# Three widths for the last two experts, and five banks for the last output rows, in an attention and MoE kernel

## The chip, the cores and the metric

The kernel runs on one core of a Trainium2 chip. A core has five engines with an instruction stream each: TensorE (PE), VectorE (DVE), ScalarE (ACT), GpSimd (POOL) and SyncE (SP), beside DMA engines. Matmuls write to PSUM, in banks of 128 partitions x 512 words of 32 bits. The metric is the device time of one execution in microseconds. Three timed runs of the kernel before gave 481.39, 474.83 and 478.11 us; the median is 478.11.

## The reference

Two parts. First an attention over 4 batches, 8 heads, 576 positions and 64 dimensions each: the sum of an attention over keys averaged by fours, and of an attention within a band of seven positions. Its output is `x`, 4 x 576 tokens of 512 values. Then a mixture of experts with one expert for each token:

```
for b in range(B):
    for s in range(S):
        e = argmax(logits[b, s]) if s == 0 or local_gate[b, s] < 0.5 else prev_e
        p = softmax(logits[b, s])
        h = maximum(x[b, s] @ w1[e], 0)        # 512 -> 1024
        out[b, s] = p[e] * (h @ w2[e])         # 1024 -> 512
        prev_e = e
```

There are 8 experts and 2,304 tokens. How many tokens an expert gets depends on the data. All of it is in fp32.

## The kernel before

The attention writes `x` to DRAM and the routing makes lists of tokens. Then come nine passes, one for each slot, in the order 0, 8, 1, 2, ..., 7. Slot 0 holds expert 0's tokens of the first three batches, slot 8 those of the last, and slots 1 to 7 the other experts, sorted by their number of tokens, most first. Slot 7 is the last pass, and has the fewest. Counted from the reference's inputs, slots 1 to 7 have 397, 330, 291, 274, 269, 214 and 165 tokens.

A product of fp32 matrices is done as three products of parts: `h` is the number rounded to the engine's fp32r, `l` the rest, and the three are h·h, h·l and l·h. ScalarE makes `h`, VectorE or GpSimd makes `l`.

One pass, say for slot e:

- SyncE loads the expert's `w1` and `w2`, ScalarE, VectorE and GpSimd split them (`conv`, L1067 and L1072). GpSimd gathers the slot's tokens in tiles of 128 rows, PE transposes them (L1119).
- First product, `mm1` (L1183): the hidden layer transposed, 8 column blocks `f` of 128 hidden units. A block is 12 matmuls into one PSUM bank, each with a weight tile of 128 x 128 and with n tokens as columns. ScalarE takes `hh` out of the bank (L1192, Relu), VectorE `hl` (L1196), which frees the bank.
- Second product, for all slots but 8 and the last, `mm2t` (L1289): the output transposed, 4 blocks of 24 matmuls, again n columns wide. VectorE copies it to `oT` (L1297), and PE transposes it back by tiles of 128 tokens (L1306) into banks of kind O.
- For slot 8 and the last slot, 7, the second product is `mm2` (L1329): rows of 128 tokens x 512, 24 matmuls for each tile, in a branch on whether the tile has any token. An empty tile runs one tiny matmul instead (`idle`, L1076, 128 x 4).
- `gated`: ScalarE scales a tile into `ot` (L1265), and GpSimd writes its rows to the output by an indirect DMA (L1269). This is done for every tile, empty ones too.

How wide n is, PE decides at run time. `LEAVES` lists the widths of each slot, and `sized` (L1162) makes a binary tree of branches on the token count whose leaves hold the matmuls for one width each. The program has such a tree for every two column blocks of the first product and for every block of the transposed second.

PSUM has five banks of kind H, for the transposed tokens and both column products, and two of kind O, for output tiles. `xcount` hands out the banks of a kind in turn, in the order in which the program records the work. A list scheduler (`order`) then sets the order of the instructions on every engine, by the cost of the path behind an operation and a priority of its slot. Each engine executes its list in order, with semaphores between the engines; an instruction that waits holds up all behind it on its engine.

The last pass orders its four tiles 3, 2, 0, 1:

```
mm2(e, o + 2, range(TILES[e]) if nx is not None else (3, 2, 0, 1))
```

Of the kernel before, what the change touches and what calls it, by code (L numbers as in the profile page):

```python
# [9 lines left out]
F32 = mybir.dt.float32  # L10
# [4 lines left out]
AF = mybir.ActivationFunctionType  # L15
# [7 lines left out]
B, H, S, D = 4, 8, 576, 64  # L23
# [7 lines left out]
ZROW = S * SPLIT // NT  # L31
SD = S // 4
LEAVES = [(256, 320, 384), (368, 400, 448, 512), (336, 368, 400, 512), (304, 336, 368, 512), (288, 304, 336, 512),
          (256, 288, 320, 512), (256, 272, 304, 512), (256, 272, 288, 512)]
TILES = [3, 4, 4, 4, 4, 4, 4, 4, 2]
NP = 120
THR = float(np.float32(-1.5 * 2.0 ** -23))
# [268 lines left out]
def attn_moe_kernel(ctx: ExitStack, tc: tile.TileContext, q, k, v, wg, wl, w1, w2, cst, idc, out, info=None):  # L306
    nc = tc.nc
    V, A, G, T, SY = nc.vector, nc.scalar, nc.gpsimd, nc.tensor, nc.sync
# [66 lines left out]
    def t(key):  # L375
        if key not in tiles:
            tag = key[0]
            if tag == "row":
                tiles[key] = pools["row0"][(2 * key[1] + key[2]) % 2]
            elif tag == "vw":  # L380
                tiles[key] = pools["vwb"][(2 * key[1] + key[2]) % 2]
            elif tag == "bd":
                tiles[key] = pools["bdb"][(2 * key[1] + key[2]) % 2]
            elif tag == "psr":
                tiles[key] = pools["psr"]
            elif tag == "ps":
                tiles[key] = pools["ps"].tile([128, 512], F32, tag=f"b{pl.bank_of[key]}", name="ps")
            else:
                sh, dt, bufs = spec[{"h0": "w1h", "w2": "w2r"}.get(key[1], tag)]
                tiles[key] = pools[gof[tag]].tile(sh, dt, tag=tag, name=tag, bufs=bufs)  # L390
        return tiles[key]
# [11 lines left out]
    gi = const.tile([128, 4, NV, 4], U32, name="gi")  # L403
# [24 lines left out]
    def apart(ins, group):  # L428
        tc.declare_no_dep(ins.ins, group=group, reason="rows are disjoint")
        tc.add_to_no_dep_group(group, ins.ins)  # L430
# [592 lines left out]
    def pk_(e, nm, x):  # L1023

        if e == 0 and nm + x in ("w1h", "w2r"):
            return ("w2r", "h0") if nm == "w1" else ("w1r", "w2")
        return (nm + x, e)

    def part(e, nm, x):
        return t(pk_(e, nm, x))  # L1030
# [44 lines left out]
    def idle():  # L1075
        T.matmul(pools["psr"][:, 448:452], wm, wm[:, 0:4], start=True, stop=True)  # L1076

    def half(e):
        return "A" if e == 0 else "B"
# [60 lines left out]
    def xcount(g, kind, n):  # L1140
        if g not in seen:
            seen[g] = bankn[kind] % n
            bankn[kind] += 1
        return seen[g]

    def mb(kind, g):
        return pools[kind][seen[g]]
# [109 lines left out]
                                    t(("hh", e))[:, 4 * q:4 * q + 4, 128 * tl:128 * tl + 128].bitcast(F32), ALU.subtract)  # L1257
                op("DVE", 602, prio + 0.2, lo, R=[g, sl, ("hhp", e, 2 * tl + q)], U=[("hh", e)], W=[("hl", e), ("hlt", e, tl)])

    def gated(e, tl, g, sl, prio):  # L1260

        ok = ("ot", e, tl)

        def ev():
            A.activation(t(ok), mb("O", g), AF.Copy, scale=gi[:, tl, e, 2:3].bitcast(F32))  # L1265
        op("ACT", 580, prio, ev, R=[g, sl, ("gi", half(e))], W=[ok])

        def st():
            ins = G.indirect_dma_start(out, bass.IndirectOffsetOnAxis(ap=gi[:, tl, e, 1:2], axis=0), t(ok), None,  # L1269
                                       bounds_check=NTOK - 1, oob_is_err=False)  # L1270
            apart(ins, "out")
        op("Pool", 1050, prio, st, R=[ok], W=[("out", e, tl)], lat=3000)

    def mm2t(e, prio, tprio):
# [24 lines left out]
        for tl in range(TILES[e]):  # L1299
            g = ("ps2", "o", e, tl)  # L1300
            sl = ("ps2f", "O", xcount(g, "O", 2))

            def tr(tl=tl, g=g):
                def go():
                    for db in range(4):
                        T.transpose(mb("O", g)[:, 128 * db:128 * db + 128], t(ok)[:, db, 128 * tl:128 * tl + 128], ident)  # L1306
                if tl < 2:
                    go()
                    return
                with tc.If(regs[e] > 128 * tl) as cmp:  # L1310
                    go()
                with cmp.Else():
                    idle()
            op("PE", 430, tprio + 0.1 * tl, tr, cnt=1024, R=[ok, ("reg", e)], W=[g, sl])
            gated(e, tl, g, sl, tprio + 0.1 * tl)

    def mm2(e, prio, tiles_):
        for n, tl in enumerate(tiles_):
            g = ("ps2", "o", e, tl)
            sl = ("ps2f", "O", xcount(g, "O", 2))  # L1320

            def fn(tl=tl, g=g):
                hh, hl = t(("hh", e)), t(("hl", e))
                wh, wlo = part(e % E, "w2", "h"), part(e % E, "w2", "l")
                with tc.If(regs[e] > 128 * tl) as cmp:
                    i = 0
                    for f in range(8):
                        for a, c in ((hh, wh), (hh, wlo), (hl, wh)):
                            T.matmul(mb("O", g), a[:, f, 128 * tl:128 * tl + 128], c[:, f], start=(i == 0), stop=(i == 23))  # L1329
                            i += 1  # L1330
                with cmp.Else():
                    idle()
            hd = [("hht", e, tl), ("hlt", e, tl)] if e == 8 else [("hh", e), ("hl", e)]
            op("PE", 5150 if tl < TILES[e] - 1 else 100, prio + 0.1 * n, fn, cnt=12000, most=0, U=[("hh", e), ("hl", e)],
               R=hd + [pk_(e % E, "w2", "h"), pk_(e % E, "w2", "l"), ("reg", e)], W=[g, sl, ("ord", seq_.index(e))])

            gated(e, tl, g, sl, prio + 0.1 * n)

    seq_ = [0, 8, 1, 2, 3, 4, 5, 6, 7]
    load_w1(0, 117)  # L1340
# [12 lines left out]
    for i, e in enumerate(seq_):  # L1353
        o = M + 10 * i
        nx = seq_[i + 1] if i + 1 < NV else None
        if nx is not None:
            if i:
                load_w1(nx, o)
            if i > 1:
                load_w2(nx, o + 0.1)  # L1360
            if i == 0:
                gather(8, 134)
                gather(1, 134.5)
            elif i > 1:
                gather(nx, o)
            count(nx, o - 9)
        (mm1x if e == 8 else mm1)(e, o)
        if i == 1:
            load_w2(nx, o + 0.1)
        if nx is not None:  # L1370
            x_T(nx, o + 1)
            if i:
                conv(nx, "w1", o + 2)
        if e < E and nx is not None and 1:
            mm2t(e, o + 2, o + 10.05)
        else:
            mm2(e, o + 2, range(TILES[e]) if nx is not None else (3, 2, 0, 1))
        if nx is not None and i:
            conv(nx, "w2", o + 4)
# [77 lines left out]
```

## Time and profile before

| | |
|---|---|
| median of three timed runs | 478.11 us (474.83 to 481.39) |
| profiled execution, its own time | 473.6 us |
| its span | 471.8 us |
| mean granted clock of TensorE | 0.943 |
| PE busy | 410.7 us, 87% |
| DVE, ACT, POOL busy | 62%, 54%, 48% |
| slot 6's second product, first to last matmul | about 415.65 to 427.22 us |
| slot 7's first product | 427.22 to 439.43 us |
| slot 7's output rows, tiles 0 and 1 | 442.01 to 455.0 us |
| last store of the passes | 456.09 us |

The busy shares are means over the whole span, with stages of different limits. What the change touches lies in the last fifth, so the timeline and the tables by stage of that part are the ones to read. Idle time of an engine is followed in brackets by what ended it, as far as the profile could tell. Matmuls are pipelined: the length shown for one is longer than the distance to the start of the next, and the distance is what counts.

### The profile page before, as it was taken

The page shows a single profiled execution, that of the slowest core. Times are in us where ns is not written, and L with a number is a line of the kernel's source. Part 1 is how long each engine was busy: PE and PEld are TensorE (multiplying, and loading weights), DVE is VectorE, ACT ScalarE, POOL GpSimd, SP SyncE. Part 2 cuts the span into 40 slices and gives each one's busy share as a digit, 9 for nine tenths or more (in the row PEclk, how much of TensorE's full clock was granted, in tenths as well). Part 3 has the DMA queues.
Part 4 walks back from the last instruction along what each step waited for, and adds up shares of the span by engine and source line. Part 5 has one row for each costly group of instructions (what it writes and reads, how often), then busy time and mean ns, then how long its engine had stood idle before and what let it go on. Part 6 is the DMA issues. An engine that isn't in the chain of part 4 may idle for free.

```text
span 471.8 us, 13009 instructions
## 1 busy us (share of the span) xinstructions
PE 410.7 (87%) x5211; PEld 379.0 (80%) x5211; DVE 291.6 (62%) x522; ACT 256.4 (54%) x526; POOL 228.8 (48%) x220
## 2 busy tenths in 40 slices
PE   5878769886999987969999999999989999989850
PEld 5867648674877876969899999999989999889640
DVE  0259296884799878662485655665677757777200
ACT  4836587773768542504645355456447564576310
POOL 4233848537677785280486521723717524153410
PEclk8879898997899998989999999999999999999895
DMA  9999895969359044364489535466463763520100
GB/s 223 207 192 202 207 184 93 215 123 197 105 181 190 6 107 101 146 125 197 140 264 360 157 134 202 139 185 245 143 256 122 247 226 131 197 91 4 42 34 1
DMA packets 77548, 74.58 MB, mean 158 GB/s; under 512 B 36162, under 2 KB 59330, under 8 KB 77444
## 3 DMA queue, kind: packets, MB, share of 16 engines
q1 hardware_dynamic: 71524, 59.66, 47.3%
q0 software_dynamic: 5920, 13.42, 9.5%
q8 instruction: 78, 1.28, 1.2%
q14 instruction: 26, 0.21, 0.2%
HBM read 63.58 MB, written 13.74 MB: 164 GB/s over the span
## 4 chain that ended last, share of the span: by engine, by line
PE 48%; issue 15%; DVE 13%; DMA 8%; POOL 7%; ACT 5%; SPq 0%; POOLq 0%; DVEq 0%; ACTq 0%
PE H L1289 16%; PE H L1183 16%; DMA ld<-in_k_dram 4%; PE ps L521 2%; POOL idp L920 2%; DMA xw<-x 2%; DMA vds<-in_v_dram 2%; DVE w2l L1072 2%; POOL out_dram L1269 1%; DVE hl L1196 1%; PE O L1306 1%; PE H L1119 1%; PE H L1217 1%; PE O L1329 1%; PE ps L641 1%
## 5 line engine op out<-in xcount | busy, mean ns | idle before, releaser
L1269 POOL DMA_INDIRECT out_dram<-ot,gi x33 | 35.9, 1088 | 84.9 <-ACT ot L1265 79.3
L1289 PE MATMUL H<-hh,w2h 128*128 128x288 f32 (+5 forms) x224 | 70.5, 315 | 6.0 <-DVE hl L1196 4.2
L1183 PE MATMUL H<-xh,w1h 128*128 128x288 f32 (+4 forms) x224 | 68.4, 305 | 2.1 <-DVE w2l L1072 1.3
L1289 PE MATMUL H<-hl,w2h 128*128 128x288 f32 (+5 forms) x224 | 69.3, 309 | 0.0
L1289 PE MATMUL H<-hh,w2l 128*128 128x288 f32 (+5 forms) x224 | 69.2, 309 | 0.0
L1183 PE MATMUL H<-xh,w1l 128*128 128x288 f32 (+4 forms) x224 | 67.9, 303 | 1.1 <-issue 1.1
L1183 PE MATMUL H<-xl,w1h 128*128 128x288 f32 (+4 forms) x224 | 67.7, 302 | 0.0
L1192 ACT ACTIVATE hh<-H 128x512 fp32r<-128x512 f32 (+1 forms) x64 | 36.4, 583 | 42.7 <-PE H L1183 40.9
L1067 ACT CAST w2h<-w2r 128x512 fp32r<-128x512 f32 x56 | 30.5, 617 | 48.5 <-issue 32.4
L1196 DVE SCALAR_TENSOR_TENSOR hl<-H,hh 128x512 fp32r<-128x512 f32 (+1 forms) x64 | 40.9, 666 | 24.4 <-ACT hh L1192 24.4
L1289 PEld LDWEIGHTS H<-hh,w2h 128*128 128x128 f32 x224 | 42.8, 191 | 7.1 <-issue 4.5
L1183 PEld LDWEIGHTS H<-xh,w1h 128*128 128x128 f32 x224 | 42.1, 188 | 3.0 <-DVE w2l L1072 1.5
L1297 DVE COPY oT<-H 128x512 f32<-128x512 f32 (+1 forms) x28 | 18.3, 668 | 41.5 <-PE H L1289 32.5
L1183 PEld LDWEIGHTS H<-xh,w1l 128*128 128x128 f32 x224 | 42.1, 188 | 1.3 <-issue 1.3
L1289 PEld LDWEIGHTS H<-hl,w2h 128*128 128x128 f32 x224 | 42.8, 191 | 0.0
L1289 PEld LDWEIGHTS H<-hh,w2l 128*128 128x128 f32 x224 | 42.7, 191 | 0.0
L1072 DVE TENSOR_TENSOR w1l<-w1r,w1h 128x512 fp32r<-128x512 f32 x41 | 38.1, 990 | 6.7 <-ACT hh L1252 6.3
L1183 PEld LDWEIGHTS H<-xl,w1h 128*128 128x128 f32 x224 | 42.1, 188 | 0.0
L1103 POOL DMA_INDIRECT xs<-xw,gi x33 | 36.6, 1108 | 11.0 <-issue 7.7
L1072 DVE TENSOR_TENSOR w2l<-w2r,w2h 128x512 fp32r<-128x512 f32 x42 | 36.5, 920 | 7.3 <-ACT w2h L1067 7.3
L1072 POOL TENSOR_TENSOR w2l<-w2r,w2h 128x512 fp32r<-128x512 f32 x14 | 20.5, 1486 | 29.7 <-ACT w2h L1067 29.7
L426 PEld LDWEIGHTS <-wm 128*128 128x128 bf16 x711 | 28.0, 107 | 6.8 <-issue 4.9
(167 smaller groups left out, 955.1 us busy)
## 6 DMA issues: line engine op xcount, KB each, us to landing
w1r<-in_moe_w_dram SPq DMA_DIRECT2D x36, 512.0 KB
w2r<-in_moe_w_dram SPq DMA_DIRECT2D x28, 512.0 KB
vds<-in_v_dram SPq DMA_DIRECT2D x8, 576.0 KB
ld<-in_q_dram SPq DMA_DIRECT2D x8, 512.0 KB
ld<-in_k_dram SPq DMA_DIRECT2D x8, 512.0 KB
xw<-x SPq DMA_DIRECT2D x16, 240.0 KB
vwb<-in_v_dram SPq DMA_DIRECT2D x31, 120.0 KB
vwb<-in_v_dram SPq DMA_DIRECT2D x31, 72.0 KB
```

The source lines that it names most:

```text
L426: T.matmul(o[:, 448:512], wm, wm[:, 0:64], start=True, stop=True)
L521: T.transpose(g[:, c, r], t(("sp", b, nm, c))[:, r, 128 * u:128 * u + 128], ident)
L920: ins = G.indirect_dma_start(idp, bass.IndirectOffsetOnAxis(ap=t(sk)[0:w, tl:tl + 1], axis=0), idt[0:w, NT * b + t0 + tl], None, bounds_ch ...
L1067: A.copy(sl("h"), sl("r"))
L1072: (G if on else V).tensor_tensor(sl("l"), sl("r"), sl("h").bitcast(F32), ALU.subtract)
L1103: ins = G.indirect_dma_start(xs_(e, tl), None, xw[0:n + 1], bass.IndirectOffsetOnAxis(ap=gi[:, tl, e, 0:1], axis=0), bounds_check=n, oob_i ...
L1183: T.matmul(hp[:, 0:n], a[:, kk, 128 * f:128 * f + 128], c[:, kk, 0:n], start=(i == 0), stop=(i == 11))
L1192: A.activation(t(("hh", e))[:, f, 0:n], mb("H", g)[:, 0:n], AF.Relu)
L1196: V.scalar_tensor_tensor(t(("hl", e))[:, f, 0:n], mb("H", g)[:, 0:n], 0.0, t(("hh", e))[:, f, 0:n].bitcast(F32), ALU.max, ALU.subtract)
L1269: ins = G.indirect_dma_start(out, bass.IndirectOffsetOnAxis(ap=gi[:, tl, e, 1:2], axis=0), t(ok), None, bounds_check=NTOK - 1, oob_is_err= ...
L1289: T.matmul(mb("H", g)[:, 0:n], a[:, f, 128 * db:128 * db + 128], c[:, f, 0:n], start=(i == 0), stop=(i == 23))
L1297: (V.tensor_copy if eng == "D" else A.copy)(t(ok)[:, db, 0:nt], mb("H", g)[:, 0:nt])
```

## The change

Slots 6 and 7 get three widths instead of four, 224, 264, 512 and 192, 256, 512. In `mm2`, and in `gated` for it, the last slot takes its banks from the five of kind H instead of the two of kind O; slot 8 keeps the O banks.

```diff
-          (256, 288, 320, 512), (256, 272, 304, 512), (256, 272, 288, 512)]
+          (256, 288, 320, 512), (224, 264, 512), (192, 256, 512)]
...
-    def gated(e, tl, g, sl, prio):
+    def gated(e, tl, g, sl, prio, kd="O"):
...
-            A.activation(t(ok), mb("O", g), AF.Copy, scale=gi[:, tl, e, 2:3].bitcast(F32))
+            A.activation(t(ok), mb(kd, g), AF.Copy, scale=gi[:, tl, e, 2:3].bitcast(F32))
...
     def mm2(e, prio, tiles_):
         for n, tl in enumerate(tiles_):
             g = ("ps2", "o", e, tl)
-            sl = ("ps2f", "O", xcount(g, "O", 2))
-
-            def fn(tl=tl, g=g):
+            kd = "O" if e == 8 else "H"
+            sl = ("ps2f", kd, xcount(g, kd, 5 if kd == "H" else 2))
+
+            def fn(tl=tl, g=g, kd=kd):
...
-                            T.matmul(mb("O", g), a[:, f, 128 * tl:128 * tl + 128], c[:, f], start=(i == 0), stop=(i == 23))
+                            T.matmul(mb(kd, g), a[:, f, 128 * tl:128 * tl + 128], c[:, f], start=(i == 0), stop=(i == 23))
...
-            gated(e, tl, g, sl, prio + 0.1 * n)
+            gated(e, tl, g, sl, prio + 0.1 * n, kd)
```

PE's program goes from 8,538 to 8,226 rows. The order of VectorE and SyncE stays; on PE, ScalarE and GpSimd it changes at the end, as follows.

On PE, at the last pass's output rows. The number behind a name tells the buffers apart (`hh_10423` is the hidden layer of slot 7, `O1_3543` the O bank 1), and in brackets stand the semaphores that an instruction waits for. Before, the last matmul of tile 2, its branches with the tiny matmul of an empty tile, and the beginning of tile 0:

```order
L1329 MATMUL O0_3542<-w2h_10311,hl_10428 128x512 [waits DVE_49]
L1325 UNCONDITIONAL_BRANCH
L1076 LDWEIGHTS wm_70
L1076 MATMUL psr_96<-wm_70 128x4
L1325 UNCONDITIONAL_BRANCH
L1325 COMPARE_AND_BRANCH
L1329 MATMUL O1_3543<-w2h_10311,hh_10423 128x512 [waits Activation_49]
L1329 MATMUL O1_3543<-w2l_10314,hh_10423 128x512
L1329 MATMUL O1_3543<-w2h_10311,hl_10428 128x512
L1329 MATMUL O1_3543<-w2h_10311,hh_10423 128x512
```

With the change, the beginning of the output rows, which is tile 0 in bank H2:

```order
L1310 UNCONDITIONAL_BRANCH
L1326 COMPARE_AND_BRANCH
L1330 MATMUL H2_3539<-w2h_10086,hh_10173 128x512 [waits DVE_49,Activation_49]
L1330 MATMUL H2_3539<-w2l_10089,hh_10173 128x512
L1330 MATMUL H2_3539<-w2h_10086,hl_10178 128x512
L1330 MATMUL H2_3539<-w2h_10086,hh_10173 128x512 [waits Activation_49]
```

Tiles 3 and 2 came before tile 0 and now follow tile 1, in banks H0 and H1; the four tiles' order on PE is 0, 1, 3, 2, and tile 1 has bank H3. A tile in an H bank waits for `hh` once for each column block, where the tile in O1 waits once, for ScalarE's `ot` of tile 3 out of that bank.

On ScalarE, the end of its list. `H3_3540` and `H4_3541` are the last two column blocks of slot 7's first product; the first two `ot` are slot 6's tiles 2 and 3. Before (the last four are slot 7's tiles 3, 2, 0, 1):

```order
L1192 ACTIVATE hh_10423<-H3_3540 128x512
L1192 ACTIVATE hh_10423<-H4_3541 128x512
L1265 ACTIVATE ot_10673<-O1_3543,gi_63 128x512
L1265 ACTIVATE ot_10676<-O0_3542,gi_63 128x512
L1325 UNCONDITIONAL_BRANCH
L1265 ACTIVATE ot_10733<-O1_3543,gi_63 128x512
L1325 UNCONDITIONAL_BRANCH x2
L1265 ACTIVATE ot_10767<-O0_3542,gi_63 128x512
L1325 UNCONDITIONAL_BRANCH
L1265 ACTIVATE ot_10798<-O1_3543,gi_63 128x512
L1265 ACTIVATE ot_10803<-O0_3542,gi_63 128x512
```

With the change (the last four are slot 7's tiles 0, 3, 1, 2):

```order
L1192 ACTIVATE hh_10173<-H3_3540 128x512
L1265 ACTIVATE ot_10371<-O1_3543,gi_63 128x512
L1192 ACTIVATE hh_10173<-H4_3541 128x512
L1265 ACTIVATE ot_10378<-O0_3542,gi_63 128x512
L1326 UNCONDITIONAL_BRANCH x4
L1265 ACTIVATE ot_10436<-H2_3539,gi_63 128x512
L1265 ACTIVATE ot_10493<-H0_3537,gi_63 128x512
L1265 ACTIVATE ot_10498<-H3_3540,gi_63 128x512
L1265 ACTIVATE ot_10500<-H1_3538,gi_63 128x512
```

One `ot` of slot 6 moved ahead of the last `hh`, and `ot` of tile 3 stands ahead of that of tile 1, though PE runs tile 1 first.

On GpSimd, the last stores follow the same order. Before (slot 6's tiles 2 and 3, then slot 7's 3, 2, 0, 1):

```order
L1269 DMA out_0_dram<-ot_10673,gi_63 2304x512
L1325 UNCONDITIONAL_BRANCH x2
L1269 DMA out_0_dram<-ot_10676,gi_63 2304x512
L1325 UNCONDITIONAL_BRANCH
L1269 DMA out_0_dram<-ot_10733,gi_63 2304x512
L1325 UNCONDITIONAL_BRANCH
L1269 DMA out_0_dram<-ot_10767,gi_63 2304x512
L1269 DMA out_0_dram<-ot_10798,gi_63 2304x512
L1269 DMA out_0_dram<-ot_10803,gi_63 2304x512
```

With the change (slot 6's tiles 2 and 3, then slot 7's 0, 3, 1, 2):

```order
L1269 DMA out_0_dram<-ot_10371,gi_63 2304x512
L1269 DMA out_0_dram<-ot_10378,gi_63 2304x512
L1326 UNCONDITIONAL_BRANCH x4
L1269 DMA out_0_dram<-ot_10436,gi_63 2304x512
L1269 DMA out_0_dram<-ot_10493,gi_63 2304x512
L1269 DMA out_0_dram<-ot_10498,gi_63 2304x512
L1269 DMA out_0_dram<-ot_10500,gi_63 2304x512
```

The stores of the empty tiles 3 and 2 stood ahead of tile 0's and now stand around tile 1's.

## Rows read from the trace of the kernel before

**Rows 1.** The page, parts 1 and 4: busy time, and the chain that ended last
```profile
PE 410.7 (87%) x5211; PEld 379.0 (80%) x5211; DVE 291.6 (62%) x522; ACT 256.4 (54%) x526; POOL 228.8 (48%) x220
...
PE 48%; issue 15%; DVE 13%; DMA 8%; POOL 7%; ACT 5%; SPq 0%; POOLq 0%; DVEq 0%; ACTq 0%
```

**Rows 2.** Table by stage: stretch, us, PE busy (count), granted clock, DMA share, GB/s
```profile
415.65:427.22 11.57, 11.57 (x97) 1.00 0.10 34
427.22:439.43 12.21, 12.21 (x106) 1.00 0.11 40
...
442.01:445.76 3.75, 3.75 (x9) 0.54 0.07 11
```

**Rows 3.** PE timeline: start, us, what, count [idle before and its releaser]; spacing
```profile
411.81 1.04 PE L1306 MATMUL O<-cs,oT 128*128 128x128 f32 x8
412.68 1.04 PE L1119 MATMUL H<-cs,xs 128*128 128x128 f32 x8
...
427.22 0.28 PE L1183 MATMUL H<-xh,w1h 128*128 128x256 f32 x1
...
432.79 0.29 PE L1183 MATMUL H<-xh,w1l 128*128 128x256 f32 x1
```

**Rows 4.** Groups by shape, PE, from 200 us: count, busy us, mean ns, idle before
```profile
L1183 PE MATMUL H<-xh,w1h 128*128 128x256 f32 x64 | 18.2, 284 | 0.1
...
L1289 PE MATMUL H<-hh,w2h 128*128 128x256 f32 x32 | 9.2, 286 | 1.4 <-ACT ot L1265 1.4
```

**Rows 5.** PE timeline in slot 6's first product
```profile
400.60 0.28 PE L1183 MATMUL H<-xl,w1h 128*128 128x256 f32 x1
401.97 0.39 PE L1183 MATMUL H<-xh,w1l 128*128 128x256 f32 x1 [1.09 <-issue]
```

**Rows 6.** The line of the trees, 403 to 406 and 413 to 416 us: ns min/median/max
```profile
L1162 PEldq COMPARE_BRANCH  x2: 208/1120/2033, 403.6 to 405.7; - x2
...
L1162 PEldq COMPARE_BRANCH  x2: 208/800/1393, 413.8 to 415.3; - x2
```

**Rows 7.** PE timeline, slot 6's second product and slot 7's output rows
```profile
414.05 0.17 PE L1076 MATMUL psr<-wm 128*128 128x4 bf16 x1
415.65 0.36 PE L1289 MATMUL H<-hh,w2h 128*128 128x256 f32 x1 [1.43 <-ACT ot L1265]
...
439.31 0.28 PE L1183 MATMUL H<-xh,w1l 128*128 128x256 f32 x1
439.43 0.25 PE L1076 MATMUL psr<-wm 128*128 128x4 bf16 x4
442.01 0.61 PE L1329 MATMUL O<-w2h,hh 128*128 128x512 f32 x1 [2.32 <-ACT ot L1265]
...
445.40 0.52 PE L1329 MATMUL O<-w2h,hl 128*128 128x512 f32 x1
...
449.28 0.39 PE L1329 MATMUL O<-w2h,hh 128*128 128x512 f32 x1
...
454.64 0.40 PE L1329 MATMUL O<-w2h,hl 128*128 128x512 f32 x1
```

**Rows 8.** ACT timeline, the first `ot` at the end
```profile
440.12 1.84 ACT L1265 ACTIVATE ot<-O,gi 128x512 f32<-128x512 f32 x3
```

**Rows 9.** DVE timeline in slot 7's first product
```profile
432.73 1.28 DVE L1196 SCALAR_TENSOR_TENSOR hl<-H,hh 128x512 fp32r<-128x512 f32 x2
...
437.44 0.69 DVE L1196 SCALAR_TENSOR_TENSOR hl<-H,hh 128x512 fp32r<-128x512 f32 x1 [0.44 <-ACT hh L1192]
...
440.26 0.69 DVE L1196 SCALAR_TENSOR_TENSOR hl<-H,hh 128x512 fp32r<-128x512 f32 x1
```

**Rows 10.** POOL timeline, the stores at the end
```profile
441.08 0.98 POOL L1269 DMA_INDIRECT out_dram<-ot,gi  x1 [3.71 <-ACT ot L1265]
442.37 0.98 POOL L1269 DMA_INDIRECT out_dram<-ot,gi  x1 [0.30 <-issue]
...
456.09 0.98 POOL L1269 DMA_INDIRECT out_dram<-ot,gi  x1 [4.62 <-ACT ot L1265]
```

## The prediction

> **What bounds the kernel now.** The page comes first. TensorE (PE) is busy for 87% of the span and holds 48% of the chain of work that ended last [rows 1]. The change touches only the last two passes, so the second view is the table by stage there: in the 24 us of slot 6's transposed second product and slot 7's first product PE is busy without a gap at full clock, with the DMA engines at about 10% [rows 2]. What ends a stage here is thus PE's own rate. The third view is PE's timeline, read for two things: how far apart the starts of neighbouring matmuls lie, and where PE stands still. Those 48 starts from 427.22 to 432.79 us have 47 intervals of 118 ns each [rows 3]. PE stands still at three places: 401.97, 415.65 and 442.01 us [rows 5, 7]. Last comes GpSimd (POOL): its store at 456.09 us is the last work of the passes [rows 10], and some 14.7 us of loads and the end of the program follow, which the change leaves alone.
>
> **The change, part by part.**
>
> *Widths.* Counting the reference's tokens gives 214 for slot 6 and 165 for slot 7, so both now run 256 columns wide (the row shapes say so too [rows 4]) and will run 224 and 192. Affected are 96 matmuls in slot 6's first product, 96 in its second and 96 in slot 7's first: 288. Slot 7's output rows stay 512 wide. Is the interval proportional to the width? If so, 118 ns become 103 (224/256) and 88 (192/256). The nearest narrower row that is also fp32 and loads a fresh weight tile each time is the run of 128-wide transposes: 8 starts from 411.81 to 412.68 us, 109 ns each [rows 3]. Half the width saves only 9 ns there. I take 109 ns for both widths, because those rows lie on the same engine at the same clock: 288 x 9 ns = 2.6 us. Below, a width could give nothing (0); above, proportion would give 192 x 15 + 96 x 30 = 5.8 us, of which the banks below leave 5.3. [...]
>
> What covers a faster PE: VectorE's `hl` frees each bank of the first product. In slot 7 column block 5 takes the bank of block 0; `hl` of blocks 0 and 1 starts at 432.73 us and takes 1.28 for both, so that bank is free at about 433.4 [rows 9], while PE reaches block 5 at about 434.7. The slack is 1.3 us, and it shrinks by 5 x 12 x 9 ns = 0.5. In proportion it would shrink by 60 x 30 ns = 1.8 and PE would wait 0.5; that is taken off the upper bound above. The conversions of weights on VectorE stand in the same queue and don't move.
>
> *Trees.* The tree of widths loses a leaf and the smallest leaf stands behind one compare instead of two. The compare itself took 208 ns and is hidden. But two branches in slot 6 took 1,393 and 2,033 ns [rows 6], and behind them PE stood still for 1.09 us at 401.97 (named "issue") and for 1.43 us at 415.65 [rows 7]. The page names `ot` for the second, but that matmul needs only `hh` and `hl` of this slot, done before; I read both as the engine waiting for its instructions. From the last matmul before to the next: 400.60 to 401.97 is 1.37, less one interval, 1.25 us; 414.05 to 415.65 is 1.60, less the 0.17 of the short matmul, 1.43 us. Together 2.7. PE's program gets 312 rows shorter, all in these two slots, so less has to be jumped over, but where the blocks of instructions end moves too. Bounds: all of it goes (+2.7) or stalls of half this size come in addition elsewhere (-1.4); I take half, 1.3 us, between them, nearer the gain because there are fewer instructions to jump over. [...]
>
> *Banks of the output rows.* Before, the four tiles run in the order 3, 2, 0, 1 in two O banks; the first two are empty. Tile 0 waits until `ot` of tile 3 has been read out of O1. The last matmul of the first product starts at 439.31 and ends its place at 439.43 [rows 7]; tile 0 starts at 442.01. With H banks its first matmul waits only for the first `hh` and for the bank H2, which `hl` of block 5 frees at 437.44 + 0.7 = 438.1 us [rows 9]. So tile 0 can start at about 439.6: 2.4 us. The order of waits confirms that later column blocks are waited for one by one; the last block's `hl` ends at 440.95 [rows 9], and its `hh`, now one `ot` (0.6 us) later on ScalarE [rows 8], is wanted only at matmul 22, 21 x 233 ns = 4.9 us after the start. If the start had to wait for that last `hl`, 1.0 us would be left: the lower bound.
>
> *Clock.* [...] The matmuls' starts lie (445.40 - 442.01)/8 = 424 ns apart, against (454.64 - 449.28)/23 = 233 ns in tile 1 [rows 7]. Tile 0 took 449.28 - 442.01 = 7.27 us, where 24 x 233 ns would be 5.6: 1.7 us. Without the standstill I expect the high level throughout, as after the 1.4 us standstill at 415.65, behind which the clock stayed at 1.00 [rows 2, 7]. Bounds: 0 to 1.7; I take 1.7.
>
> *The tail.* This part costs. ScalarE now reads the output tiles in the order 0, 3, 1, 2 and POOL stores them so. Tiles 3 and 2 are empty, but an empty tile's store occupies POOL as long as another: 0.98 us, next start 442.37 - 441.08 = 1.29 us later [rows 10]. Before, both lay beside tile 0's matmuls. Now tile 3's stands ahead of tile 1's store, and it cannot be early, because its `ot` waits for PE's branch that comes after tile 1's matmuls; tile 2's stands behind. POOL is what ends last there: 2 x 1.29 = 2.6 us lost. ScalarE's extra `ot` runs beside the first store. Bounds: 1.3 if only the store behind counts, 2.9 with a branch and a short matmul ahead (four of those took 0.25 us [rows 7]).
>
> **The sum.** 2.6 + 1.3 + 2.4 + 1.7 - 2.6 = 5.4 us, made against the profiled execution: 473.6 becomes 468.2. That execution lies under the median of the three timed runs, 478.11 (474.83 to 481.39), so I subtract the same 5.4 us there: 472.7 us, 1.1% less.
>
> **The rivals.**
> 1. *Widths pay in proportion*, no floor: 5.3 - 2.6 = 2.7 us more, 470.0. For it: the interval of 512-wide matmuls, 233 ns, is about twice the 118 of 256-wide ones, so width is what is paid there. Against it: the transposes' 109 ns.
> 2. *The interval stays at 118 ns*: 2.6 us less gain, 475.3. For it: 118 is near the 109 already.
> 3. *The instruction stalls move and grow* by 1.4 us rather than shrink by 1.3: 475.4. For it: a branch of 2,033 ns beside one of 208 on one line shows that position decides, and all later positions move.
> 4. *Slower*: narrower matmuls leave PE partly idle, and the granted clock falls to its lower level in slots 6 and 7. There a matmul takes 424/233 = 1.83 times as long for its columns, 189 ns at 224 wide and 162 at 192. Against 118 that loses 192 x 71 + 96 x 44 ns = 17.8 us, and with the other terms (2.8) 478.1 + 17.8 - 2.8 = 493.1. It decides as soon as about 45 of the 288 matmuls run so (45 x 62 ns = 2.8 us), and it takes 200 for over 2%. For it: the low level did occur, at 442.01. Against it: there PE had stood still; the transposes with 109 ns and stalls of 1.4 us left the level high [rows 2, 3, 7].
> 5. *The change doesn't do what it says*: a count above 224 or 192 would send a slot to 264 or 256 columns. Then the widths give about -0.8 instead of 2.6: 476.1. The counts of the seeded inputs speak against it.
>
> **How the numbers follow.** Forecast 0.60, rival 1 0.15, rival 2 0.10, rival 3 0.09, rival 4 0.04, rival 5 0.02. The predicted time is the forecast's, 472.7. The forecast's own bounds, with the unknown terms not all at one end, and the medians' spread of 0.7% each way (taken at half, since it is a median) give 469 to 477; rivals 1 to 3 and 5 fall inside 467.5 to 478.5, which is the range. About 2% is what a measurement of this kernel can tell from no change. Faster than that is below 468.5: a third of rival 1 (0.05) and 0.04 of the forecast, 0.09. Slower, above 487.7, is most of rival 4: 0.03. The rest is 0.88.
>
> **What would show it.** Right: matmul starts 109 ns apart in both products of slot 6 and in the first of slot 7; the first output row's matmul within 0.4 us of the last one of the first product; granted clock 1.00 there and 233 ns intervals from the first on; two POOL stores around tile 1's in the tail, the last starting some 2.6 us after the earliest moment that tile 1's own could; no branch of over 1 us in slot 6, or one. Wrong: intervals near 103 and 88 ns (rival 1) or 118 (rival 2); new standstills ahead of a tree's first matmul (rival 3); a granted clock of about a half (rival 4); rows 264 wide (rival 5). The forecast also fails if the stores of empty tiles turn out shorter in the tail than they were, or if VectorE's `hl` is late for a bank.

## The result: 1.05% faster, and the profile after

Twenty runs each gave medians of 473.82 us (468.08 to 482.32) with the change and 483.98 us before. The ratio is 0.9895, with a 95% interval of 0.9847 to 0.9943; it compares the means of those runs that lie within 1.5% of the fastest of their kernel (472.08 us of twelve, 477.09 us of eight), and is therefore not the quotient of the two medians, 0.979. So the kernel became faster by 0.6 to 1.5%. The prediction's 472.7 us and its 1.1% lie close by, and 473.82 lies in its range, but its statement that about 2% is what a measurement can tell from no change is wrong.

The profiled execution took 471.83 us, its span 470.0. The first view is the page's busy line, beside [rows 1]:

```profile
PE 410.5 (87%) x5211; PEld 377.3 (80%) x5211; DVE 286.8 (61%) x522; ACT 256.4 (55%) x526; POOL 230.3 (49%) x220
```

It tells nothing: the shares are the same within a point. Nor does the span, since slot 6 began at 398.72 us in the profile before and at 403.20 in this one, in work that the change doesn't touch. Over all profiles of this study that start lies between 398.0 and 416.8 us, for kernels of either kind. So I measure from the first matmul of slot 6 to the start of the last store: 456.09 - 398.72 = 57.37 us before, 52.16 after. What follows the last store isn't the same in the two, though: 471.8 - 456.09 = 15.7 us before, 470.0 - 455.36 = 14.6 after. To the end of the span the gain is thus 6.3 us and not 5.2. The experiment with the empty tiles first takes that up.

The table by stage of the changed kernel, in the columns of [rows 2] (slot 6's second product, slot 7's first product, the first 3.75 us of the output rows, the rest of them):

```profile
416.38:428.62 12.24, 11.15 (x97) 1.00 0.32 117
428.62:440.19 11.57, 11.57 (x106) 1.00 0.11 41
440.25:444.00 3.75, 3.75 (x19) 1.00 0.02 2
444.00:451.50 7.50, 7.50 (x34) 1.00 0.13 43
```

The granted clock is 1.00 throughout, where the third line was 0.54. In PE's timeline, the first two rows below are the first and last of slot 6's first product (96 matmuls, 224 wide), then 48 of slot 7's (192 wide), then the one standstill left, and the passage to the output rows:

```profile
403.20 0.27 PE L1183 MATMUL H<-xh,w1h 128*128 128x224 f32 x1
...
413.80 0.28 PE L1183 MATMUL H<-xh,w1l 128*128 128x224 f32 x1
...
428.62 0.26 PE L1183 MATMUL H<-xh,w1h 128*128 128x192 f32 x1
...
433.86 0.28 PE L1183 MATMUL H<-xh,w1l 128*128 128x192 f32 x1
...
420.58 0.27 PE L1289 MATMUL H<-hh,w2h 128*128 128x224 f32 x1
421.94 0.37 PE L1289 MATMUL H<-hl,w2h 128*128 128x224 f32 x1 [1.09 <-issue]
...
440.07 0.27 PE L1183 MATMUL H<-xh,w1l 128*128 128x192 f32 x1
440.19 0.20 PE L1076 MATMUL psr<-wm 128*128 128x4 bf16 x2
440.25 0.48 PE L1330 MATMUL H<-w2h,hh 128*128 128x512 f32 x1
...
451.30 0.40 PE L1330 MATMUL H<-w2h,hl 128*128 128x512 f32 x1
```

(413.80 - 403.20)/95 = 111.6 ns at 224 columns and (433.86 - 428.62)/47 = 111.5 ns at 192. Tile 0 starts 0.18 us after the last matmul of the first product, where it was 2.70 [rows 7], and the 47 intervals of the output rows are (451.30 - 440.25)/47 = 235 ns from the start. The end on ScalarE and GpSimd, beside [rows 8, 10]:

```profile
451.82 1.84 ACT L1265 ACTIVATE ot<-H,gi 128x512 f32<-128x512 f32 x3 [4.99 <-PE psr L1076]
```

```profile
447.10 0.98 POOL L1269 DMA_INDIRECT out_dram<-ot,gi  x1 [3.40 <-ACT ot L1265]
452.78 0.98 POOL L1269 DMA_INDIRECT out_dram<-ot,gi  x1 [4.70 <-ACT ot L1265]
454.07 0.98 POOL L1269 DMA_INDIRECT out_dram<-ot,gi  x1 [0.30 <-issue]
455.36 0.99 POOL L1269 DMA_INDIRECT out_dram<-ot,gi  x1 [0.30 <-issue]
```

The last three stores are those of tile 3 (empty), tile 1 and tile 2 (empty). Tile 1's could have started by 452.78, where tile 3's did: both come from the same run of `ot`.

### The profile page after: what moved, and what is told of

It reads as the page before. It is cut to its first block, busy times and chain, and to the rows that moved or that the text cites. A ratio compares the mean times of both kernels' runs of the same rounds, so it can differ in the third digit from the quotient of the medians.

```text
span 470.0 us, 12998 instructions
## 1 busy us (share of the span) xinstructions
PE 410.5 (87%) x5211; PEld 377.3 (80%) x5211; DVE 286.8 (61%) x522; ACT 256.4 (55%) x526; POOL 230.3 (49%) x220
## 3 DMA queue, kind: packets, MB, share of 16 engines
q8 instruction: 76, 1.25, 1.2%
## 4 chain that ended last, share of the span: by engine, by line
PE 59%; issue 13%; DVE 12%; DMA 5%; ACT 5%; POOL 2%; SPq 1%; POOLq 0%; DVEq 0%; ACTq 0%
PE H L1183 18%; PE H L1289 18%; PE ps L688 3%; DMA ld<-in_q_dram 2%; PE ps L521 2%; PE ps L426 2%; PE H L1119 2%; DMA vds<-in_v_dram 2%; PE ps L641 2%; PE ps L772 1%; DVE w2l L1072 1%; PE O L1306 1%; DMA xw<-x 1%; PE psr L426 1%; PE H L1217 1%
## 5 line engine op out<-in xcount | busy, mean ns | idle before, releaser
L1183 PE MATMUL H<-xh,w1h 128*128 128x288 f32 (+5 forms) x224 | 67.6, 302 | 2.5 <-DVE w2l L1072 2.5
L1183 PE MATMUL H<-xl,w1h 128*128 128x288 f32 (+5 forms) x224 | 67.2, 300 | 0.0
L1183 PE MATMUL H<-xh,w1l 128*128 128x288 f32 (+5 forms) x224 | 67.2, 300 | 0.0
L1072 DVE TENSOR_TENSOR w1l<-w1r,w1h 128x512 fp32r<-128x512 f32 x41 | 34.9, 910 | 7.6 <-ACT hh L1252 6.3
L688 PE MATMUL ps<-T 64*32 64x32 f32 x1536 | 23.1, 205 | 13.1 <-issue 13.1
```

Source lines behind the costliest of these rows:

```text
L688: T.matmul(sv(hb)[32 * h4:32 * h4 + 32, w], t(qT)[r0:r0 + 64, pr, c0:c0 + 32], t(kT)[r0:r0 + 64, pr, c0:c0 + 32], start=True, stop=True)
L1072: (G if on else V).tensor_tensor(sl("l"), sl("r"), sl("h").bitcast(F32), ALU.subtract)
L1183: T.matmul(hp[:, 0:n], a[:, kk, 128 * f:128 * f + 128], c[:, kk, 0:n], start=(i == 0), stop=(i == 11))
```

## Experiments

The numbers of the stages, in us, from one profile for each execution. The columns: from slot 6's first matmul to its second product; from there to slot 7's first; from there to tile 0; from tile 0's first matmul to the start of the last store; the sum of these four; and from the start of the last store to the end of the span.

| kernel | slot 6, first | slot 6, second | slot 7, first | tile 0 to last store | sum | last store to end |
|---|---|---|---|---|---|---|
| before | 16.93 | 11.57 | 14.79 | 14.08 | 57.37 | 15.7 |
| before, again | 15.02 | 12.03 | 14.79 | 12.52 | 54.36 | 15.9 |
| before, third | 15.95 | 12.16 | 14.85 | 14.05 | 57.01 | 15.9 |
| banks only | 14.10 | 12.12 | 12.27 | 15.12 | 53.61 | 14.6 |
| banks only, again | 15.48 | 11.92 | 12.34 | 15.11 | 54.85 | 14.7 |
| matmuls in the standstill | 14.19 | 12.41 | 14.86 | 12.51 | 53.97 | 16.0 |
| widths only | 13.32 | 11.21 | 14.14 | 14.06 | 52.73 | 15.8 |
| widths only, again | 13.19 | 11.67 | 14.14 | 14.06 | 53.06 | 16.0 |
| changed | 13.18 | 12.24 | 11.63 | 15.11 | 52.16 | 14.6 |
| changed, again | 13.17 | 11.13 | 11.63 | 15.10 | 51.03 | 14.5 |
| changed, third | 13.28 | 11.00 | 11.63 | 15.11 | 51.02 | 14.8 |
| changed, fourth | 13.33 | 11.20 | 11.63 | 15.11 | 51.27 | 14.6 |
| empty tiles first | 13.28 | 11.00 | 11.68 | 12.49 | 48.45 | 15.9 |
| the same, again | 13.17 | 11.15 | 11.68 | 12.50 | 48.50 | 15.9 |
| the same, third | 13.16 | 11.31 | 11.68 | 12.49 | 48.64 | 15.7 |
| one width | 12.99 | 10.92 | 11.63 | 15.10 | 50.64 | 14.5 |
| four widths | 14.37 | 12.17 | 11.63 | 15.11 | 53.28 | 14.6 |
| four widths, again | 14.07 | 11.96 | 11.63 | 15.11 | 52.77 | 14.4 |

**The banks alone.**

```diff
-          (256, 288, 320, 512), (224, 264, 512), (192, 256, 512)]
+          (256, 288, 320, 512), (256, 272, 304, 512), (256, 272, 288, 512)]
```

> The H banks for the last pass's output rows, with the four old widths. Measured from slot 6's first matmul of the first product to the start of the last store: 57.37 us before, 51.83 with the whole change. Theory (each part of the change acts by itself): the rows start at once (2.2 us), at the high clock (1.7 us), and two stores of empty tiles stand around tile 1's (+2.6): 57.37 - 3.9 + 2.6 = 56.1 us; matmuls 118 ns apart, both stalls of over 1 us in slot 6 still there. Rival (the tail hides the stores, or the widths are needed for an early start): 53.5, or 57 and more. Of the whole time about -1.3 us, ratio 0.997.

The 51.83 us of this expectation and of the one on the empty tiles were counted from slot 6's fourth matmul; from its first they are 52.16. The passage to tile 0 (0.18 us), the clock (1.00) and the tail (15.12 us) came as expected. The sum was 53.61, not 56.1, mostly because the standstills in slot 6 were small in this execution (0.41 and 0.47 us). That broke the expectation that both would be there, and led to the repetitions below. Ratio 0.989 (0.9828 to 0.9953).

**The widths alone**, on the kernel before.

```diff
-          (256, 288, 320, 512), (256, 272, 304, 512), (256, 272, 288, 512)]
+          (256, 288, 320, 512), (224, 264, 512), (192, 256, 512)]
```

> The three widths, with the O banks of before. Theory: 288 matmuls each 6.9 ns closer together (118.5 to 111.6 ns) give 2.0 us, and one of the two stalls in slot 6 goes (1.4 us): 57.37 - 3.4 = 54.0 us from slot 6's first matmul to the last store; the standstill of 2.3 us before tile 0 and its first matmuls 424 ns apart stay; the last store of all is tile 1's. Rival (the stall goes because of the code's position, which the banks alter too): both stalls back, 55.4 us, or none, 52.8. Ratio about 0.993.

52.73 us. Slot 6's first product is 13.32, slot 7's is 0.65 us shorter (14.14 against 14.79), and the standstill ahead of tile 0 (2.33 us idle) and its slow start (a granted clock of 0.61 in the first 3.75 us) stayed. No standstill of over 0.2 us was left in slot 6, the rival's 52.8. Ratio 0.9962 (0.9897 to 1.0028).

**The empty tiles first**, on the changed kernel.

```diff
         for n, tl in enumerate(tiles_):
+            if n == 0:
+                p0 = prio
+            prio = p0 - 150 * (e == 7 and tl > 1)
             g = ("ps2", "o", e, tl)
```

> The whole change, with the empty tiles 3 and 2 ordered ahead of tiles 0 and 1 on TensorE, ScalarE and GpSimd, as before the change. Theory (the two stores around tile 1's cost their full 2 x 1.29 us): 51.83 - 2.6 = 49.2 us from slot 6's first matmul to the last store, which is tile 1's; tile 0's first matmul still within 0.4 us of the first product's last. Rival 1: the empty tiles' matmul and branch ahead of tile 0 wait for the last hidden block, so that tile 0 starts 1 us or more later at a low clock: 51 to 52. Rival 2: the end is set by something else than GpSimd's stores: 51.8. Ratio to the kernel before about 0.984.

48.45 us, 3.7 below the changed kernel. The theory has 2.6 of them; the rest is mostly the standstill at 421.94, which this execution didn't have. The stores on GpSimd (tiles 3, 2, 0, 1 of slot 7 from the first row on; tile 1's is the last):

```profile
446.55 0.99 POOL L1269 DMA_INDIRECT out_dram<-ot,gi  x1 [0.30 <-issue]
447.84 0.98 POOL L1269 DMA_INDIRECT out_dram<-ot,gi  x1 [0.30 <-issue]
449.74 0.98 POOL L1269 DMA_INDIRECT out_dram<-ot,gi  x1 [0.91 <-ACT ot L1265]
455.33 0.98 POOL L1269 DMA_INDIRECT out_dram<-ot,gi  x1 [4.62 <-ACT ot L1265]
```

The two empty stores now lie beside tile 0's matmuls, and the stage from tile 0 to the last store is 12.49 instead of 15.11 us: the prediction's 2.6 us. Tile 0 started 0.23 us after the last matmul, so the empty tiles ahead of it cost 0.05. Ratio 0.9805 (0.9695 to 0.9916).

But only half of the 2.6 us reaches the end of the program. The spans, of the changed kernel and of this one:

```profile
span 470.0 us, 12998 instructions
```

```profile
span 471.2 us, 13001 instructions
```

From tile 1's store to the end it is 471.8 - 456.09 = 15.7 us in the kernel before, 470.0 - 454.07 = 15.9 in the changed one and 471.2 - 455.33 = 15.9 here. In all twenty profiles of this study it is 15.7 to 16.1 us, whether tile 2's store follows or not. So the store behind tile 1's cost nothing here; the one ahead of it, tile 3's, cost its 1.29 us. What the end of the program waits for in those 15.7 us the views don't name. To the end, this order gains 1.6 us over the changed kernel, on the mean of three executions and four.

**Matmuls in the standstill**, on the kernel before.

```diff
+                if e == 7 and tl == 0:
+                    for _ in range(20):
+                        T.matmul(pools["psr"][:, 0:128], wm, wm, start=True, stop=True)
                 with tc.If(regs[e] > 128 * tl) as cmp:
```

> The kernel before, with 20 matmuls of 128 x 128 that nobody reads on TensorE just ahead of tile 0 of the last output rows, in the time in which it stood still. Theory (the standstill of 2.3 us is what makes the granted clock fall): tile 0 starts when it did, its matmuls lie 233 ns apart instead of 424 for the first nine, and tile 0 takes 5.6 us instead of 7.3: 55.7 us from slot 6's first matmul to the last store. Rival (the start of the 512-wide rows itself brings the low clock, or the bank's wait): the nine at 424 ns stay, 57.4.

PE's timeline and the table by stage of this kernel:

```profile
446.75 1.28 PE L1327 MATMUL psr<-wm 128*128 128x128 bf16 x20
449.22 0.50 PE L1332 MATMUL O<-w2h,hh 128*128 128x512 f32 x1 [1.19 <-ACT ot L1265]
```

```profile
449.22:452.97 3.75, 3.75 (x16) 1.00 0.07 11
```

Tile 0 was released as late as before (2.70 us), and had a granted clock of 1.00 at once; from tile 0 to the last store 12.51 instead of 14.08 us, the theory's 1.6. The sum was lower than expected (53.97) through slot 6 alone. The kernel before, repeated, weakens this as a proof, since it once had 1.00 without any filling; this kernel ran with a profile only once.

**Both kernels again**, unchanged.

> The kernel before, unchanged, in another execution with a profile. Theory (the two standstills of 2.7 us together in slot 6 are this execution's and not the code's): they differ by over 1 us in sum; the standstill ahead of tile 0 (2.7 us from the last matmul) and tile 0's low clock are there again within 0.1 us. Rival (the code's position sets them): again about 1.1 and 1.4 us in the same two places.

> The changed kernel in another execution with a profile. Theory (as for the kernel before): the standstill of 1.1 us in slot 6's second product moves or goes; the intervals of 111.6 ns, the start of tile 0 0.18 us after the last matmul, and the three stores at the end 1.29 us apart stay. Rival: the standstill is at the same matmul with the same length.

> The kernel before, a third execution with a profile. Theory: the standstill ahead of tile 0 is 2.7 us again; whether the granted clock falls behind it and how long TensorE waits for instructions in slot 6 differ from one execution to the next (so far 0.54 and 1.00; 2.7 and 0.8 us).

> The changed kernel, a third execution with a profile. Theory: 111.6 ns, tile 0 0.18 us after the last matmul of the first product, 15.1 us from tile 0 to the last store, as in both before; the standstills in slot 6 between 0 and 1.1 us.

The kernel before, again (PE's timeline and its table by stage), and then its third execution:

```profile
427.82 0.36 PE L1289 MATMUL H<-hh,w2h 128*128 128x256 f32 x1 [0.42 <-issue]
431.30 0.38 PE L1289 MATMUL H<-hh,w2h 128*128 128x256 f32 x1 [0.34 <-issue]
...
454.64 0.50 PE L1329 MATMUL O<-w2h,hh 128*128 128x512 f32 x1 [2.33 <-ACT ot L1265]
```

```profile
454.64:458.40 3.76, 3.76 (x16) 1.00 0.06 11
```

```profile
451.08:454.83 3.75, 3.75 (x11) 0.62 0.07 11
```

The bank's standstill of 2.7 us is there every time. The clock behind it is not low every time: 0.54, 1.00 and 0.62, and 0.61 and 0.64 in the two executions with the widths alone. So four of five executions with that standstill began the rows at a clock of 0.54 to 0.64, and none of the twelve in the table in which tile 0 followed within 0.3 us did: there tile 0's first eight intervals were 244 or 245 ns on the mean, against 424 in the profile before, and the clock was 1.00 in the three whose table was read. My expectation that the low clock would be there again was wrong. Nor do the standstills in slot 6 have a fixed length. Of the pair of 1.09 and 1.43 us [rows 5, 7], the first was gone in both repetitions; the second, ahead of slot 6's second product, was there with 0.42 and 0.81 us. There were others, of up to 1.09 us, at the first matmul of a tree. The changed kernel had its 1.09 us at 421.94 in one of four executions only.

**One width**, on the changed kernel (it fits counts up to 224 and 192).

```diff
-          (256, 288, 320, 512), (224, 264, 512), (192, 256, 512)]
+          (256, 288, 320, 512), (224,), (192,)]
```

> The whole change with a single width for slots 6 and 7, 224 and 192: no tree and no jump there (it fits only counts up to these, as the reference's inputs have). Theory (TensorE's standstills of 0.4 to 1.4 us in slot 6 come from jumping over leaves): none is left in slots 6 and 7; slot 6's first matmul to its second product 13.1 us, from there to slot 7 11.0 instead of 12.24, and 50.9 us instead of 52.16 from slot 6's first matmul to the last store. Rival (they come when the program is being loaded, straight on too): a standstill of 0.4 us or more remains in slot 6 or 7, 51.5 or more.

No standstill was left in slots 6 and 7: 12.99 and 10.92 us, 50.64 in sum, where the theory has 13.1, 11.0 and 50.9. Ratio 0.9909 (0.9848 to 0.997).

**Four widths, as narrow**, on the changed kernel.

```diff
-          (256, 288, 320, 512), (224, 264, 512), (192, 256, 512)]
+          (256, 288, 320, 512), (224, 264, 304, 512), (192, 256, 288, 512)]
```

> The whole change with a fourth width put back, 224, 264, 304, 512 and 192, 256, 288, 512: the smallest leaf still 224 and 192 columns, but the trees as long as before. From slot 6's first matmul to its second product six executions with the old trees took 14.10 to 16.93 us, nine with three leaves 13.16 to 13.33, one with one leaf 12.99. Theory A (the length of the trees makes TensorE wait for instructions): 13.5 to 16 us. Theory B (the narrower matmuls or something else does it): 13.2 us.

> The same kernel in a second execution with a profile, since the waits differ from one to the next. Theory A: 13.5 to 16 us from slot 6's first matmul to its second product. Theory B: 13.2 us.

14.37 and 14.07 us for slot 6's first product where three widths took 13.16 to 13.33, and the sum is 53.28 and 52.77 against 51.02 to 52.16. PE's standstills in the first of the two, each at the first matmul of a tree:

```profile
404.95 0.37 PE L1183 MATMUL H<-xh,w1h 128*128 128x224 f32 x1 [0.46 <-DVE w2l L1072]
...
413.35 0.34 PE L1289 MATMUL H<-hh,w2h 128*128 128x224 f32 x1 [0.47 <-DVE xl L1134]
...
417.38 0.37 PE L1289 MATMUL H<-hh,w2h 128*128 128x224 f32 x1 [1.11 <-DVE oT L1297]
```

The engines named as releasers are different for each; what goes with the standstills is the fourth leaf, which nobody executes. Theory A's time holds for slot 6 (13.5 to 16 us); slot 7's first product took 11.63 us with one, three and four widths alike. That PE waits for instructions there isn't shown. The fourth leaf also puts a second compare ahead of the smallest one, and no run tells the longer code from that compare.

**64 and 128 columns**, on the changed kernel, in both products of the trees.

```diff
                 def go(n):
+                    n = {224: 64, 192: 64}.get(n, n) if e > 5 else n
```

> The whole change with 64 columns instead of 224 and 192 in the smallest leaf of slots 6 and 7 (the other tokens' hidden values and outputs are left out). Theory (a floor that the width doesn't set): matmuls stay 109 to 112 ns apart in both products of slot 6 and the first of slot 7. Rival 1 (proportion): about 30 ns. [...] A low clock would show as more than 112.

> The whole change with 128 columns instead of 224 and 192 in the smallest leaf of slots 6 and 7 (the other tokens' hidden values and outputs are left out). With 64 columns the interval was 111.6 ns at the high clock, and the granted clock fell to 0.50 some 6 us into slot 6's first product, with 213 ns from there on. Theory A (the prediction's fourth rival; the narrower the matmuls, the sooner the clock falls): it falls with 128 as well, 213 ns for most of the 288 matmuls, the whole some 25 us longer than the changed kernel. Theory B (128 columns still hold the clock, like 192 and 224): 111.6 ns all through, granted clock 1.00.

With 64 columns, PE's timeline shows pairs of rows ten intervals apart, first at a granted clock of 1.00 and then at 0.50, and the table by stage shows the granted clock of these stretches:

```profile
418.90 0.28 PE L1184 MATMUL H<-xh,w1l 128*128 128x64 f32 x1
420.01 0.28 PE L1184 MATMUL H<-xh,w1h 128*128 128x64 f32 x1
...
424.14 0.40 PE L1184 MATMUL H<-xh,w1h 128*128 128x64 f32 x1
426.27 0.40 PE L1184 MATMUL H<-xl,w1h 128*128 128x64 f32 x1
```

```profile
416.75:422.00 5.25, 5.25 (x50) 1.00 0.74 265
422.86:432.00 9.14, 9.14 (x44) 0.50 0.66 231
439.20:475.00 35.80, 35.80 (x172) 0.51 0.06 20
```

The weight loads at 0.50, in PE's other timeline:

```profile
424.29 0.33 PEld L1184 LDWEIGHTS H<-xl,w1h 128*128 128x128 f32 x1
424.50 0.33 PEld L1184 LDWEIGHTS H<-xh,w1l 128*128 128x128 f32 x1
424.71 0.33 PEld L1184 LDWEIGHTS H<-xh,w1h 128*128 128x128 f32 x1
```

They lie 0.21 us apart, as the matmuls do. With 128 columns, 80 intervals and the stage:

```profile
402.23 0.22 PE L1184 MATMUL H<-xh,w1h 128*128 128x128 f32 x1
...
411.11 0.28 PE L1184 MATMUL H<-xh,w1l 128*128 128x128 f32 x1
```

```profile
402.30:413.00 10.70, 10.70 (x98) 1.00 0.45 163
```

At a clock of 1.00 the interval is 111 ns at 64 and at 128 columns, and 111.5 and 111.6 at 192 and 224: a floor, and from 64 to 224 columns the width doesn't set it. At 64 columns the granted clock fell from 1.00 to 0.50, with PE busy for all of both stretches, and the interval became 213 ns; that run took 509.43 us. At 128 it stayed at 1.00, and the run took 470.19 us. Each is one execution. Theory B of the second run holds for 128. What the prediction's fourth rival warned of, a granted clock of about a half with narrower matmuls, was seen at 64 columns (0.50) and in no execution with 128, 192 or 224.

**The parts timed side by side.**

> The H banks with the old widths once more, beside the widths alone, the whole change and the empty tiles first. By the stages of three profiles of the kernel before and three of the changed one: the earlier start of the rows 2.5 us and on the mean 1.0 of clock against 2.6 of stores: 0.9 us, ratio 0.998. Rival (the earlier 0.989 holds; the banks alone carry the gain): 0.989.

> The widths with the O banks once more. By the stages: 288 x 6.9 ns = 2.0 us, and 1.4 to 1.9 us of standstills in slot 6 that the longer trees had on the mean: 3.4 to 3.9 us, ratio 0.992. Rival (the earlier 0.996): half of that.

> The whole change once more. By the stages 56.25 - 51.40 = 4.9 us on the mean of three profiles each: ratio 0.990.

> The whole change with the empty tiles first, a second time, for a closer ratio. By the stage (48.45 us from slot 6's first matmul to the last store, against 51.03 and 52.16 of the changed kernel and 54.36 and 57.37 of the kernel before): 0.983 to 0.988 of the kernel before. Rival (the earlier 0.9805 was luck of three runs and the empty tiles make no difference): 0.9895 as the changed kernel.

> The whole change with the empty tiles first, a third time. By the stages 2.5 to 2.6 us below the changed kernel: ratio 0.984 to 0.985.

Ratios: banks alone 0.9906 (0.9822 to 0.999), widths alone 1.002 (0.9962 to 1.0077), whole change 0.9865 (0.9805 to 0.9926), empty tiles first 0.9839 (0.9689 to 0.9989) and 0.987 (0.9784 to 0.9955). The whole change is faster again. Up to the last store the banks alone gain 56.25 - 54.23 = 2.0 us and the widths alone 56.25 - 52.90 = 3.4 (means of the executions in the table). To the end of the span, by the table's last two columns, the means are 72.1 us before, 68.9 with the banks alone, 68.8 with the widths alone, 66.0 with the whole change and 64.4 with the empty tiles first. The gains are thus 3.2, 3.3, 6.1 and 7.7 us, or 0.7, 0.7, 1.3 and 1.6% of 477 us. The expected ratio of the banks, 0.998, had counted 2.6 us for the stores, which is too much. All the intervals hold these gains but one, the second timing of the widths alone (0.9962 to 1.0077). The kernels with one part alone run the same work as the kernel before up to slot 6, so I trust the stages for where time goes, but why that timing shows none of the 0.7% stays open. Whether the order with the empty tiles first is faster than the changed kernel can't be told from these ratios either.

## Why the prediction was right, and where it was wrong

**The verdict drawn from the number** is a step that failed: "About 2% is what a measurement of this kernel can tell from no change", and 0.88 on that. Twenty runs a side resolved 0.5% each way. A gain of 1.1% was thus to be called faster; the sum said so, and I did not. The chance of faster over 2% itself wasn't touched: 1.05% isn't over 2%.

**The sum**: 5.4 us forecast, with the end of the program, "which the change leaves alone", at nothing. To the end of the span the stages give 73.1 - 66.8 = 6.3 us in the pair of profiles, and 72.1 - 66.0 = 6.1 on the mean of three executions and four. By term:

- *The tail* is the other step that failed, and the term that was mis-sized most: forecast -2.6 us, measured -1.3 to the end of the program. Up to the last store the 2.6 are there (15.11 - 12.49, with and without the two stores around tile 1's). But the program ends 15.7 to 16.1 us after tile 1's store, with a store behind it or without, so what follows the last store got shorter, from 15.7 to 14.6 us in the pair. Only the store ahead of tile 1's costs. The prediction's lower bound, 1.3, was the right number for the wrong one of the two stores.
- *Widths*, forecast 2.6 us: 288 x (118.5 - 111.6) = 2.0. The floor was right; the 109 ns of the transposes [rows 3] were a little too low for it. Rivals 1 and 2 fall. What sets the floor isn't shown: in the 64-column run, at a clock of 0.50, the weight loads came 0.21 us apart, as the matmuls did, and no run took the loads away.
- *Trees*, forecast 1.3 us between -1.4 and +2.7: four leaves with the new widths cost 53.03 - 51.37 = 1.7 us more than three, on the mean. For the standstills at a tree's first matmul in slot 6 the number of leaves did matter: one leaf leaves none, and a fourth one that isn't executed brings 0.46, 0.47 and 1.11 us. That PE waits there for its instructions was the author's reading, and no run shows it. Of blocks of instructions the pages show only the packets of an instruction queue (`q8 instruction: 78, 1.28, 1.2%` before, `q8 instruction: 76, 1.25, 1.2%` after): an estimated 1.28 MB / 78 = 16.4 KB each, and two fewer with 312 rows less. One of the two that the term was made from isn't of that kind, as the lines below show. It was also wrong to treat the two standstills of one profile as the code's: they come and go between executions of one kernel, and only their mean belongs to the change. Rival 3 falls.
- *Banks*, forecast 2.4 us: 2.70 - 0.18 = 2.5, in every execution. The order of waits told it.
- *Clock*, forecast 1.7 us. In the profile before, the granted clock was 0.50 from 443.00 to 445.40 us and 1.00 from 445.80 to 446.50: a low and a high level. The stages give 12.63 - 11.05 = 1.6 from tile 0's first matmul to the last one of tile 1, in two of the kernel before's three executions, and 0 in one, so 1.1 on the mean. The prediction's bounds had the 0; it took the one profile for all.

PE's timeline of the kernel before, around the branch of 2,033 ns (the two branches of [rows 6] start at 403.6 and 405.7 us), and that of the widths alone, again:

```profile
405.59 0.28 PE L1183 MATMUL H<-xh,w1l 128*128 128x256 f32 x1
405.98 0.39 PE L1183 MATMUL H<-xh,w1h 128*128 128x256 f32 x1
```

```profile
416.23 0.37 PE L1289 MATMUL H<-hl,w2h 128*128 128x224 f32 x1 [0.51 <-issue]
```

Beside that branch PE lost only 405.98 - 405.59 - 0.12 = 0.27 us. The 1.09 us at 401.97 lie ahead of it, and not behind it as the prediction read, at the 18th matmul of a leaf of 24, where nothing jumps. The standstill of the changed kernel at 421.94 lies inside a leaf too, and that of the second fence is at the same matmul. So about half of the forecast's 2.7 us wasn't a matter of trees. What such a standstill inside a leaf waits for stays open.

The errors are +1.3 (tail), -0.6, +0.4, +0.1 and -0.6, together +0.6: 6.0 us by the terms, 6.1 by the stages. That 5.4 came so close is thus partly luck, since the errors cancel; the timing alone, 2.7 to 7.3 us, can't tell 5.4 from 6.1. It is luck too that 472.7 lies so near to 473.82: it was counted from the median of three runs, 478.11, and that of the twenty is 483.98. Rival 4, slower by the clock, did not come: the granted clock was 1.00 at 224 and 192 columns in the profile after, and in the other executions with these widths the first 48 starts of each first product lay as close, 111.3 to 111.5 ns apart. Rival 5 falls: the rows are 224 and 192 wide.

## What to carry to other kernels

Cost a change by the stage that it touches, and follow it to the end of the program: a stage that ends with the last store can hide or invent a cost. Take PE's standstills and the clock behind them from several executions, since one profile's aren't the code's: the same kernel had 0.54, 1.00 and 0.62 behind the same 2.7 us. Look for what a new order puts ahead of the last useful store: the store of an empty tile took as long as a full one (0.98 us, the next 1.29 us later) and held it up, while one behind it cost nothing here. And say beside a small forecast what the measurement will resolve, from the number of runs and not from their scatter.

## What the runs showed of the hardware

- The matmuls of these products, which load a new weight tile each time, lay 111 ns apart on the mean at 64 and 128 columns and 111.5 and 111.6 at 192 and 224; at 256 they were 118.5 ns apart [rows 3]. At a granted clock of 0.50 the distance was 213 ns at 64 columns.
- With 64 columns PE's granted clock went from 1.00 (416.75 to 422.00 us) to 0.50 and 0.51 (422.86 to 432.00 and 439.20 to 475.00), with PE busy for all of these stretches; with 128 it stayed at 1.00 (402.30 to 441.00; one execution each).
- With one more leaf, never executed, and its compare in each of slot 6's eight trees (four for the first product, four for the second), the stages took 1.7 us longer (mean of two executions against four). In the four trees of slot 7 the same cost nothing (11.63 us).
- The store of an empty tile held GpSimd as long as a full one (0.98 us, the next one 1.29 us later). Behind the last useful store it left the end of the program where it was, 15.7 to 16.1 us after that store.
- After the same standstill of 2.7 us the clock was low in four of five executions (0.54, 0.61, 0.62 and 0.64 over the first 3.75 us, and 1.00 in the fifth).
